# Attention's keys in one part, or in two parts of 640 and 512

## The chip, the cores and the metric

The kernel runs on one core of a Trainium2 chip. A core has five engines that run their own instruction queues in order and signal one another: TensorE (PE: matmuls, with weight loads shown apart as PEld), VectorE (DVE), ScalarE (ACT), GpSimd (POOL) and SyncE (SP), which here only issues DMAs. Results of TensorE land in PSUM, eight banks of 512 fp32 columns on 128 partitions; everything else works in SBUF. The metric is the device time of one execution in microseconds.

## The reference

Three computations follow each other, in fp32:

```python
# attention: B 2, H 8, S 1152, D 64; queries are averaged in pairs, so 576 a head
q_pool = q.reshape(B, H, S // 2, 2, D).mean(axis=3)
scores = scale * np.matmul(q_pool, k.transpose(0, 1, 3, 2))
scores = scores - np.max(scores, axis=-1, keepdims=True)
attn = np.exp(scores)
attn = attn / (np.sum(attn, axis=-1, keepdims=True) + 1e-09)
x = np.matmul(attn, v)          # -> 1152 tokens of 512
# experts: E 4, F 1024, weighted by normed probabilities
out += p[:, e:e + 1] * (np.maximum(x @ w1[e], 0.0) @ w2[e])
# ELU feed-forward: 512 -> 2048 -> 512
g = np.where(h > 0.0, h, np.exp(np.minimum(h, 0.0)) - 1.0)
return g @ w_out
```

## The kernel before

Attention comes first, for 16 heads in 8 pairs. A pair has 2 x 576 = 1152 query rows, cut into 9 blocks of 128; the middle block holds rows of both heads. Queries and keys are split into a rounded part and a remainder, so that products in a fast matmul format keep fp32 precision. The steps have one-letter names in the code, and this document uses them:

- q, k, v: loads (SP); a, b, c: sum, rounded part and remainder of the queries; d, e: the same for keys.
- S: scores of a block, six matmuls of 384 columns into three PSUM banks (`scores`, L401). There are two such buffers, so S of a block waits for E of the block before last.
- R: the negated maximum of a row over its 1152 scores (`max_all`, L412, VectorE). E: the exponential with the row's sum (`exp`, L420, ScalarE), into one of five buffers in SBUF.
- T: three times per block, three 128x128 transposes into one of the two remaining PSUM banks (L431). D and G: the copy out of it into the buffer `pt` (L247, on ScalarE or VectorE).
- V: the product with the values, 18 matmuls of 288 columns (each recorded as two) in three groups (`values`, L453), which holds one of the two banks that the transposes use. O: the copy of its result (L247).
- I: sum plus 1e-9, and its reciprocal (L464, L465, VectorE). 3 and 4: the reciprocals go to DRAM and come back broadcast over 64 partitions (SP). X: the head's result times them (L250, GpSimd). H and L: its rounded part (ScalarE) and remainder (GpSimd), which the experts' matmuls read.

The order on each engine is written by a planner, `order_of`: it takes the steps with their needs from `attention_ops`, durations from the table `STAGES`, and a rank for each, and lays out a schedule; instructions are issued in that order. PSUM banks are given out there too. The experts and the feed-forward (L627 and the lines around it) follow with an order of their own; their first matmuls are mixed in among attention's last.

Of the kernel before, what the change touches and what calls it, by code (L numbers as in the profile page):

```python
# [18 lines left out]
P = 128  # L19
# [8 lines left out]
    "S": (dict(PE=1040), 3),  # L28
    "R": (dict(DVE=1353), 1.5),
    "E": (dict(ACT=1431), 1),  # L30
    "I": (dict(DVE=360), 3),
    "3": (dict(SP=500), 2),
    "4": (dict(SP=500), 2),
    "X": (dict(POOL=1414), 2),
    "T": (dict(PE=327), 2),
    "D": (dict(ACT=480, DVE=557), 2),
    "G": (dict(ACT=480, DVE=557), 2),
    "V": (dict(PE=1900), 2),
    "O": (dict(ACT=720, DVE=750), 1),
    "H": (dict(ACT=690), 0.5),  # L40
    "L": (dict(POOL=1414), -4),
    "a": (dict(POOL=1400), -8),
    "b": (dict(ACT=686), -8),
    "c": (dict(DVE=1400), 5),
    "d": (dict(ACT=1160), -6),
    "e": (dict(POOL=1450), 1),
# [13 lines left out]

MIXED = {"D": dict(ACT=320, DVE=330), "G": dict(ACT=320, DVE=330), "S": dict(PE=2080)}
HALVES = {"a": dict(POOL=690, DVE=373), "b": dict(ACT=375), "c": dict(DVE=373), "d": dict(ACT=575, DVE=373), "e": dict(POOL=1365, DVE=673)}
MB = 9
NP = 5
VC = 3
# [7 lines left out]
def attention_ops(NH, KC):  # L73
# [8 lines left out]
    last = ("V", KC // VC - 1)  # L82
    t = 2700
    for i in range(NH):
# [7 lines left out]
        op(b, [(last[0], i - 3, last[1])] if i > 2 else [], "v", i, after=9000)  # L92

        free = [("S", x) for x in blocks_of(i - 4)] if i > 3 else []
# [8 lines left out]
    for b in range(NB):  # L103
# [30 lines left out]
    for j in range(8):  # L134
        op(w + j, [("S", w + j)], "w", j)
# [7 lines left out]
def order_of(ops):  # L143
# [12 lines left out]
    banks, holds, end, out = {0: 0, 1: 0}, {}, {}, []  # L156

    def ns(o, e):
        return of(o)[e]

    def of(o):
        if o[0] in MIXED and o[1] % MB == 4:
# [4 lines left out]

    while ready:
        best = []
        for o, t in ready.items():  # L170
            if o[0] == "T" or (o[0] == "V" and o[2] == 0):
                if not banks:
                    continue
                t = max(t, min(banks.values()))
            _, e = min((max(t, free[e]) + ns(o, e), e) for e in of(o))
# [3 lines left out]
        free[e] = start + ns(o, e)  # L179
        end[o] = free[e] + LATE.get(o[0], LAG[e])  # L180
        bank = None
        if o[0] == "T" or (o[0] == "V" and o[2] == 0):
            bank = min(banks, key=banks.get)
            del banks[bank]
            holds[o] = bank
        elif o[0] in "DG":
            other = ("DG"[o[0] == "D"], *o[1:])
            if other not in ops or other in end:
                banks[holds[("T", *o[1:])]] = max(end[o], end.get(other, 0))
        elif o[0] == "O":  # L190
# [591 lines left out]
```

## Time and profile before

| | |
|---|---|
| time, median of 3 runs | 900.61 us (899.84 to 901.08) |
| the profiled execution | 903.94 us, its span 901.8 us |
| mean granted clock of TensorE | 0.988 |
| attention, from the profile | 0 to about 299 us |
| busy in the whole span: PE, DVE, ACT, POOL | 866.5, 463.1, 354.3, 395.5 us |

Matmuls are pipelined, and their ends in the profile are modelled: a PE that is shown busy need not be at its peak, and where matmuls follow each other the distance of their starts says more than the duration of one. A row of a group gives the busy time of its instructions, the mean of one, and the idle time of the engine just ahead of them with what ended it.

### The profile page before, as it was taken

The page shows a single profiled execution, that of the slowest core. Times are in us where ns is not written, and L with a number is a line of the kernel's source. Part 1 is how long each engine was busy: PE and PEld are TensorE (multiplying, and loading weights), DVE is VectorE, ACT ScalarE, POOL GpSimd, SP SyncE. Part 2 cuts the span into 40 slices and gives each one's busy share as a digit, 9 for nine tenths or more (in the row PEclk, how much of TensorE's full clock was granted, in tenths as well). Part 3 has the DMA queues.
Part 4 walks back from the last instruction along what each step waited for, and adds up shares of the span by engine and source line. Part 5 has one row for each costly group of instructions (what it writes and reads, how often), then busy time and mean ns, then how long its engine had stood idle before and what let it go on. Part 6 is the DMA issues. An engine that isn't in the chain of part 4 may idle for free.

```text
span 901.8 us, 13389 instructions
## 1 busy us (share of the span) xinstructions
PE 866.5 (96%) x5374; PEld 801.7 (89%) x5374; DVE 463.1 (51%) x601; ACT 354.3 (39%) x609; POOL 395.5 (44%) x278
## 2 busy tenths in 40 slices
PE   7879898989999999999999999999999999999998
PEld 6667666767766899999999999999999999999998
DVE  6737556746544155465464655564656622333333
ACT  5668667767756331312212212212223253313221
POOL 1455444364112351546455554546464573625321
PEclk8989999999999999999999999999999999999999
DMA  8586867588440522424143325233143311000011
GB/s 246 74 166 78 143 74 91 89 157 75 30 24 8 198 105 71 143 55 168 48 143 117 117 95 144 104 105 129 38 156 123 117 48 47 1 1 1 1 40 66
DMA packets 40348, 81.93 MB, mean 91 GB/s; under 512 B 14304, under 2 KB 17376, under 8 KB 37344
## 3 DMA queue, kind: packets, MB, share of 16 engines
q1 hardware_dynamic: 40288, 81.09, 38.5%
q8 instruction: 42, 0.69, 0.4%
q14 instruction: 18, 0.15, 0.1%
HBM read 70.27 MB, written 10.80 MB: 90 GB/s over the span
## 4 chain that ended last, share of the span: by engine, by line
PE 72%; DMA 12%; DVE 4%; ACT 4%; issue 3%; SPq 2%; POOL 2%; ACTq 0%; DVEq 0%; POOLq 0%
PE p L627 62%; DMA q<-in_q 7%; PE t L453 4%; PE s L401 3%; PE t L431 3%; DMA rb<-dr 2%; SPq L321 2%; ACT e L420 2%; DVE nm L412 1%; DMA dr<-sm 1%; DMA k<-in_k 1%; POOL acc L682 1%; ACT pt L247 1%; DVE pt L247 1%; DMA w<-in_wa 1%
## 5 line engine op out<-in xcount | busy, mean ns | idle before, releaser
L627 PE MATMUL p<-XH,h 128*128 128x384 f32 (+1 forms) x608 | 198.4, 326 | 0.4 <-DVE e L657 0.4
L627 PE MATMUL p<-XL,h 128*128 128x384 f32 (+1 forms) x608 | 198.3, 326 | 0.0
L627 PE MATMUL p<-XH,l 128*128 128x384 f32 (+1 forms) x608 | 198.1, 326 | 0.0
L627 PE MATMUL p<-hh,l 128*128 128x384 f32 (+1 forms) x608 | 197.9, 326 | 0.0
L627 PE MATMUL p<-hl,h 128*128 128x384 f32 (+1 forms) x608 | 197.9, 326 | 0.0
L627 PE MATMUL p<-hh,h 128*128 128x384 f32 (+1 forms) x608 | 197.9, 326 | 0.0
L250 POOL TENSOR_TENSOR l<-w,h 128x512 fp32r<-128x512 f32 x96 | 125.6, 1326 | 74.5 <-ACT h L247 73.5
L648 ACT ACTIVATE hh<-p 128x768 fp32r<-128x768 f32 (+1 forms) x50 | 39.5, 789 | 279.9 <-PE p L627 279.9
L649 DVE SCALAR_TENSOR_TENSOR hl<-p,hh 128x768 fp32r<-128x768 f32 (+1 forms) x50 | 46.3, 926 | 161.1 <-ACT hh L648 161.1
L401 PE MATMUL s<-K,Q 128*128 128x384 f32 x480 | 108.2, 365 | 16.2 <-ACT e L420 14.3
L412 DVE TENSOR_REDUCE nm<-s 128x1 f32<-128x1152 f32 x72 | 97.4, 1355 | 47.8 <-PE s L401 47.7
L627 PEld LDWEIGHTS p<-XH,h 128*128 128x128 f32 x608 | 114.1, 188 | 0.7 <-PE p L627 0.7
L627 PEld LDWEIGHTS p<-XL,h 128*128 128x128 f32 x608 | 114.1, 188 | 0.4 <-issue 0.4
L431 PEld LDWEIGHTS t<-ident,e 128*128 128x128 f32 x648 | 75.7, 144 | 43.5 <-issue 15.8
L627 PEld LDWEIGHTS p<-XH,l 128*128 128x128 f32 x608 | 114.1, 188 | 0.0
L627 PEld LDWEIGHTS p<-hh,h 128*128 128x128 f32 x608 | 114.1, 188 | 0.0
L627 PEld LDWEIGHTS p<-hl,h 128*128 128x128 f32 x608 | 114.1, 188 | 0.0
L627 PEld LDWEIGHTS p<-hh,l 128*128 128x128 f32 x608 | 114.1, 188 | 0.0
L431 PE MATMUL t<-ident,e 128*128 128x128 f32 x648 | 101.6, 285 | 13.0 <-ACT pt L247 5.0
L401 PEld LDWEIGHTS s<-K,Q 128*128 128x128 f32 x480 | 85.5, 199 | 21.7 <-ACT e L420 19.3
L601 POOL TENSOR_TENSOR nt<-nt,ne 128x512 f32<-128x512 f32 x32 | 41.8, 1307 | 121.8 <-issue 61.5
L661 POOL TENSOR_TENSOR hl<-e,hh 128x768 fp32r<-128x768 f32 (+1 forms) x26 | 44.9, 1726 | 110.2 <-ACT hh L660 110.1
(52 smaller groups left out, 987.7 us busy)
## 6 DMA issues: line engine op xcount, KB each, us to landing
w<-in_wb SPq DMA_DIRECT2D x8, 1024.0 KB, 6.5
d<-in_va SPq DMA_DIRECT2D x16, 512.0 KB, 4.5
w<-nt SPq DMA_DIRECT2D x32, 256.0 KB, 3.3
d<-in_vb SPq DMA_DIRECT2D x16, 512.0 KB, 4.2
w<-w SPq DMA_DIRECT2D x8, 1024.0 KB, 6.9
q<-in_q SPq DMA_DIRECT2D x56, 144.0 KB, 9.2
k<-in_k SPq DMA_DIRECT2D x56, 144.0 KB, 6.6
w<-in_wa SPq DMA_DIRECT2D x7, 1024.0 KB, 9.6
```

Source lines behind the costliest of these rows:

```text
L247: (nc.scalar.copy if e == "ACT" else engines[e].tensor_copy)(out, a)
L250: engines[e].tensor_tensor(out=out, in0=a, in1=b, op=op)
L321: nc.sync.dma_start(out=t[D * r : D * r + D], in_=src)
L401: nc.tensor.matmul(out=s_t[b][:, j, :KP], lhsT=q[:, x, o : o + P], rhs=ks[p % 2][:, y, KP * j : KP * j + KP], start=k == x == 0, stop=2 * ...
L412: nc.vector.tensor_reduce(out=nm[b], in_=s_t[b][:, :, :KP], axis=AX.XY, op=ALU.max, negate=True)
L431: nc.tensor.transpose(t[:, c * P : c * P + P], et[b % NP][:, (3 * u + c) * P : (3 * u + c + 1) * P], ident)
L453: nc.tensor.matmul(out=tb[i][64 * z : 64 * z + 64, :HQ], lhsT=raws[i, "v"][:, c, :], rhs=pt[i % 2][:, c, half(z)], start=c == 0, stop=c == ...
L601: nc.gpsimd.tensor_tensor(out=t, in0=t, in1=e, op=ALU.add)
L627: nc.tensor.matmul(out=ps, lhsT=w[:, c, m * P : m * P + P], rhs=x[:, c], start=c == 0 and w is hi and x is xh, stop=c == 3 and w is lo,)
L648: nc.scalar.activation(oh, s, AF.Relu)
L649: nc.vector.scalar_tensor_tensor(out=ol, in0=s, scalar=0.0, in1=f(oh), op0=ALU.max, op1=ALU.subtract)
L661: nc.gpsimd.tensor_tensor(out=ol, in0=e, in1=f(oh), op=ALU.subtract)
```

## The change

The 1152 keys are taken in two parts, the first 640 and the other 512. Each part of a block has its own scores (four matmuls of 320 columns into two banks, or two of 512 into one), its own maximum, exponential and sum, and its own PSUM buffer: two buffers of two banks and two of one, six banks as before. The exponentials of a row are thus taken against two different maxima. The values product is split by keys in the same way, into a product of ten and one of eight matmuls with results of their own, each with its own use of a bank and its own copy (O). For each row two factors are made: from the greater of the maxima (`greater`, step I), an exponential (`factors_exp`, step J on ScalarE), and the joined sum's reciprocal (`factors`, step K). They go through DRAM as the reciprocals did, two for each row, and X multiplies both results by them and adds them. The planner's durations and ranks are other ones, and the order of nearly everything in attention differs.

```diff
-    "S": (dict(PE=1040), 3),
...
+    "S": (dict(PE=585), 8),
...
+    "X": (dict(POOL=4240), 0),
...
+SECOND = {"S": dict(PE=455), "R": dict(DVE=690), "E": dict(ACT=790), "V": dict(PE=2140)}
...
-VC = 3
+CUT = 5
+BANKS = {"S0": 2, "S1": 2, "T": 2}
...
-        op(b, need + [b > 1 and ("E", b - 2)], "S", b)
-        op(b, [("S", b)], "R", b)
-        op(b, [("R", b), *[("T", b - NP, u) for u in U if b >= NP]], "E", b)
+        for z in (0, 1):
+            op(b + 0.3 * z, need, "S", b, z)
+            op(b + 0.3 * z, [("S", b, z)], "R", b, z)
+            op(b + 0.3 * z, [("R", b, z), *[("T", b - NP, u) for u in U if b >= NP]], "E", b, z)
         for u in U:
-            op(b, [("E", b)] + [(last[0], i - 2, last[1]) for i in hs if i > 1], "T", b, u)
+            op(b, [("E", b, z) for z in (0, 1) if (z == 0 and 3 * u < CUT) or (z and 3 * u + 3 > CUT)] + [("V", i - 2, 1) for i in hs if i > 1], "T", b, u)
             op(b, [("T", b, u)], "D", b, u)
...
-            for c in range(KC // VC):
-                ds = [("D", x, u) for x in blocks_of(i) for u in U if VC * c < 3 * u + 3 and 3 * u < VC * c + VC]
+            for h in (0, 1):
+                cs = range(CUT, KC) if h else range(CUT)
+                ds = [("D", x, u) for x in blocks_of(i) for u in sorted({c // 3 for c in cs})]
                 if i % 2:
                     ds = [("G", *x[1:]) if x[1] == blocks_of(i)[0] else x for x in ds]
-                op(b + 0.1 * c, ds + [("V", i, c - 1) if c else ("v", i)], "V", i, c)
-            op(b, [("V", i, KC // VC - 1)] + [("L", i - 2)] * (i > 1), "O", i)
-            op(b, [("E", b)], "I", i)
-            op(b, [("I", i), i > 1 and ("4", i - 2)], "3", i)
+                op(b + 0.5 * h, ds + [("V", i, 0) if h else ("v", i)], "V", i, h)
+                op(b + 0.5 * h, [("V", i, h)] + [("L", i - 2)] * (i > 1), "O", i, h)
+            op(b, [("E", b, 0), ("E", b, 1)], "I", i)
+            op(b, [("I", i)], "J", i)
+            op(b, [("J", i)], "K", i)
+            op(b, [("K", i), i > 1 and ("4", i - 2)], "3", i)
             op(b, [("3", i), i % 2 and ("3", i - 1), i > 1 and ("X", i - 2)], "4", i)
-            op(b, [("O", i), ("4", i)], "X", i)
+            op(b, [("O", i, 0), ("O", i, 1), ("4", i)], "X", i)
             op(b, [("X", i)], "H", i)
...
+        PARTS = [(2, CUT * P // 2), (1, (KC - CUT) * P)]
+        s_bank = [
+            [ps_s.tile([P, n, 512], F32, name="s%d%d" % (z, j)) for j in range(BANKS["S%d" % z])]
+            for z, (n, _) in enumerate(PARTS)
+        ]
...
+        st = [[mx_p.tile([P, MB, 2], F32, name="st%d%d" % (j, x), bufs=1) for x in range(3)] for j in range(2)]
+        def part(z):
+            o = CUT * P * z
+            return slice(o, o + PARTS[z][0] * PARTS[z][1])
+        def scores(e, b, z, n):
             p, m = divmod(b, MB)
-            s_t[b] = ps_s.tile([P, 3, 512], F32, tag="s", name="s")
+            s_t[b, z] = t = s_bank[z][n][:, :, : PARTS[z][1]]
             hs = [0] * (m <= MH) + [1] * (m >= MH)
-            n = 2 * len(hs)
+            last = 2 * len(hs) - 1
             q = qs[p % 2].rearrange("p x y q -> p x (y q)")
-            for j in range(3):
+            for j in range(PARTS[z][0]):
+                c = part(z).start + j * PARTS[z][1]
                 for k, y in enumerate(hs):
                     o = P * m - Q * y + QW * y
                     for x in (0, 1):
                         nc.tensor.matmul(
-                            out=s_t[b][:, j, :KP],
+                            out=t[:, j],
                             lhsT=q[:, x, o : o + P],
-                            rhs=ks[p % 2][:, y, KP * j : KP * j + KP],
+                            rhs=ks[p % 2][:, y, c : c + PARTS[z][1]],
                             start=k == x == 0,
-                            stop=2 * k + x == n - 1,
+                            stop=2 * k + x == last,
                         )
-        def max_all(e, b):
-            nm[b] = mx_p.tile([P, 1], F32, tag="nm", name="nm")
+        def max_all(e, b, z):
+            p, m = divmod(b, MB)
+            nm[b, z] = st[p % 2][0][:, m, z : z + 1]
             nc.vector.tensor_reduce(
-                out=nm[b], in_=s_t[b][:, :, :KP], axis=AX.XY, op=ALU.max, negate=True
+                out=nm[b, z], in_=s_t[b, z], axis=AX.XY, op=ALU.max, negate=True
             )
-        def exp(e, b):
+        def exp(e, b, z):
             p, m = divmod(b, MB)
-            if m == 0:
-                sm[p] = x_p.tile([P, MB], F32, tag="sm", name="sm")
             nc.scalar.activation(
-                et[b % NP].rearrange("p (j k) -> p j k", j=3),
-                s_t.pop(b)[:, :, :KP],
+                et[b % NP][:, part(z)].rearrange("p (j k) -> p j k", j=PARTS[z][0]),
+                s_t.pop((b, z)),
                 AF.Exp,
-                bias=nm.pop(b),
-                accum_out=sm[p][:, m : m + 1],
+                bias=nm.pop((b, z)),
+                accum_out=st[p % 2][1][:, m, z : z + 1],
             )
...
+        def stats(i):
+            c = slice(MH + 1, MB) if i % 2 else slice(0, MH + 1)
+            return [t[:, c] for t in st[i // 2 % 2]]
+        def greater(e, i):
+            m, _, t = stats(i)
+            tt("DVE", t[:, :, 0], m[:, :, 0], m[:, :, 1], ALU.min)
+            tt("DVE", t[:, :, 1], t[:, :, 0], m[:, :, 1], ALU.subtract)
+            tt("DVE", t[:, :, 0], t[:, :, 0], m[:, :, 0], ALU.subtract)
+        def factors_exp(e, i):
+            t = stats(i)[2]
+            nc.scalar.activation(t, t, AF.Exp)
+        def factors(e, i):
+            m, s, t = stats(i)
+            tt("DVE", s, s, t, ALU.mult)
+            nc.vector.scalar_tensor_tensor(
+                out=s[:, :, 0], in0=s[:, :, 0], scalar=1e-9, in1=s[:, :, 1], op0=ALU.add, op1=ALU.add
+            )
+            nc.vector.reciprocal(out=s[:, :, 0], in_=s[:, :, 0])
+            for z in (0, 1):
+                tt("DVE", t[:, :, z], t[:, :, z], s[:, :, 0], ALU.mult)
...
+        def values(e, i, h, n):
+            tb[i, h] = bank[n]
+            cs = range(CUT, KC) if h else range(CUT)
+            for c in cs:
                 for z in (0, 1):
                     nc.tensor.matmul(
-                        out=tb[i][64 * z : 64 * z + 64, :HQ],
+                        out=tb[i, h][64 * z : 64 * z + 64, :HQ],
                         lhsT=raws[i, "v"][:, c, :],
                         rhs=pt[i % 2][:, c, half(z)],
-                        start=c == 0,
-                        stop=c == KC - 1,
+                        start=c == cs[0],
+                        stop=c == cs[-1],
...
+        xo = x_p.tile([P, 2, Q], F32, name="xo")
+        fb = x_p.tile([P, 2 * Q], F32, name="fb")
...
+        def output(e, i, h):
+            o = tb.pop((i, h))
             for z in (0, 1):
-                copy(e, xs[i][rows(i), half(z)], o[D * z : D * z + D, :HQ])
+                copy(e, xo[rows(i), h, half(z)], o[D * z : D * z + D, :HQ])
...
+        def factors_out(e, i):
+            p, y = divmod(i, 2)
+            if y == 0:
+                rc[p] = dr_p.tile([MB, P, 2], F32, tag="dr", name="dr")
+            s = slice(MH + 1, MB) if y else slice(0, MH + 1)
+            nc.sync.dma_start(out=rc[p][s].rearrange("m p z -> p m z"), in_=stats(i)[2])
+        def factors_in(e, i):
+            p, y = divmod(i, 2)
+            d = rc[p].rearrange("m p z -> (m p z)")[2 * Q * y : 2 * Q * y + 2 * Q]
+            nc.sync.dma_start(out=fb[rows(i)], in_=d.unsqueeze(0).to_broadcast([D, 2 * Q]))
         def x_scaled(e, i):
-            tt(e, xs[i][rows(i)], xs[i][rows(i)], rc.pop((i, "b"))[rows(i)], ALU.mult)
+            x = xo[rows(i)]
+            tt(e, x, x, fb[rows(i)].rearrange("p (q z) -> p z q", z=2), ALU.mult)
+            tt(e, x[:, 0], x[:, 0], x[:, 1], ALU.add)
```

TensorE's queue around the first head's values product, before (`t_104`, `t_105` are the two banks, `e_97` to `e_101` the five buffers of exponentials, `s` a score buffer):

```order
L401 MATMUL s<-K_108,Q_106 128x384 x6
L431 MATMUL t_104<-ident,e_101 128x128 x3
L453 MATMUL t_105<-pt_102,v 64x288 x6
L431 MATMUL t_104<-ident,e_97 128x128 x3
L453 MATMUL t_105<-pt_102,v 64x288 x6
L431 MATMUL t_104<-ident,e_97 128x128 x3
L453 MATMUL t_105<-pt_102,v 64x288 x6
L431 MATMUL t_104<-ident,e_97 128x128 x3
L401 MATMUL s<-K_108,Q_106 128x384 x6
L431 MATMUL t_105<-ident,e_98 128x128 x3
L431 MATMUL t_104<-ident,e_98 128x128 x3
L401 MATMUL s<-K_109,Q_107 128x384 x6
```

And at the same head with the change (`s_106`, `s_107` are the buffers of the first part, `s_108`, `s_109` of the second):

```order
L442 MATMUL s_107<-K_112,Q_110 128x320 x4
L496 MATMUL t_105<-ident,e_97 128x128 x3
L519 MATMUL t_104<-pt_102,v 64x288 x10
L496 MATMUL t_105<-ident,e_97 128x128 x3
L442 MATMUL s_109<-K_112,Q_110 128x512 x2
L442 MATMUL s_106<-K_112,Q_110 128x320 x4
L496 MATMUL t_104<-ident,e_97 128x128 x3
L442 MATMUL s_108<-K_112,Q_110 128x512 x2
L496 MATMUL t_105<-ident,e_98 128x128 x3
L496 MATMUL t_104<-ident,e_98 128x128 x3
L442 MATMUL s_107<-K_113,Q_111 128x320 x4
L496 MATMUL t_105<-ident,e_98 128x128 x3
```

The three values groups with transposes between them are now one of ten matmuls here and one of eight further on, and scores stand in half blocks between the transposes.

VectorE's queue at the reciprocals of one head, before (`nm` the maximum, `sm` the sums):

```order
L412 TENSOR_REDUCE nm<-s 128x1 x3
L247 COPY pt_102<-t_105 128x3x128
L464 TENSOR_SCALAR sm<-sm 128x5
L465 RECIPROCAL sm<-sm 128x5
L412 TENSOR_REDUCE nm<-s 128x1 x2
```

And at the first head's factors with the change (`st_114`, `st_115`, `st_116` hold maxima, sums and factors):

```order
L278 TENSOR_TENSOR st_116<-st_114 128x5
L278 TENSOR_TENSOR st_116<-st_116,st_114 128x5 x2
L453 TENSOR_REDUCE st_114<-s_106 128x1
L275 COPY pt_102<-t_105 128x3x128
L275 COPY pt_103<-t_104 128x3x64
L453 TENSOR_REDUCE st_114<-s_108 128x1
L278 TENSOR_TENSOR st_115<-st_115,st_116 128x10
L486 SCALAR_TENSOR_TENSOR st_115<-st_115 128x5
L489 RECIPROCAL st_115<-st_115 128x5
L278 TENSOR_TENSOR st_116<-st_116,st_115 128x5 x2
```

Two instructions in one place have become eight in two groups, with ScalarE's exponential (J) between the groups.

## Rows read from the trace of the kernel before

**Rows 1.** Stretches: us, busy time (count) of each engine, PEclk, DMA share, GB/s

```profile
0.00:299.00 299.00, 267.39 (x1741) 203.08 (x1742) 170.68 (x233) 198.62 (x372) 110.89 (x84) 0.97 0.63 95
299.00:902.00 603.00, 599.12 (x3635) 598.60 (x3633) 292.40 (x368) 155.68 (x238) 284.64 (x194) 1.00 0.27 89
```

**Rows 2.** Groups of the first 299 us: busy us, mean ns | idle before, releasers

```profile
L431 PE MATMUL t<-ident,e 128*128 128x128 f32 x648 | 101.6, 285 | 13.0 <-ACT pt L247 5.0 <-DVE pt L247 3.1 <-ACT x L247 2.3
L412 DVE TENSOR_REDUCE nm<-s 128x1 f32<-128x1152 f32 x72 | 97.4, 1355 | 47.8 <-PE s L401 47.7
L420 ACT ACTIVATE e<-s,nm 128x1152 f32<-128x1152 f32 x72 | 88.0, 1225 | 4.7 <-DVE nm L412 4.0
L464 DVE TENSOR_SCALAR sm<-sm 128x5 f32<-128x5 f32 (+1 forms) x16 | 7.5, 472 | 1.7 <-ACT e L420 1.7
```

**Rows 3.** Waits (us, times, longest); then the timeline at the longest and another

```profile
PEld s L401 <- ACT e L420: 19.3, 20, 3.8
...
44.99 0.68 ACT L366 ACTIVATE Q<-q 128x576 fp32r<-128x576 f32 x1 [4.26 <-DMA q<-in_q]
...
46.93 1.54 PEld L401 LDWEIGHTS s<-K,Q 128*128 128x128 f32 x6 [3.84 <-ACT e L420]
...
275.35 1.01 PEld L401 LDWEIGHTS s<-K,Q 128*128 128x128 f32 x6 [1.19 <-ACT e L420]
```

**Rows 4.** Timeline behind a values product: start, us, instruction, idle before

```profile
221.67 1.30 PE L401 MATMUL s<-K,Q 128*128 128x384 f32 x6
...
223.01 1.36 DVE L412 TENSOR_REDUCE nm<-s 128x1 f32<-128x1152 f32 x1 [0.43 <-PE s L401]
...
223.39 1.29 PE L401 MATMUL s<-K,Q 128*128 128x384 f32 x6
...
224.66 1.22 ACT L420 ACTIVATE e<-s,nm 128x1152 f32<-128x1152 f32 x1
...
226.02 1.00 PEld L401 LDWEIGHTS s<-K,Q 128*128 128x128 f32 x6 [0.93 <-ACT e L420]
226.03 1.32 PE L401 MATMUL s<-K,Q 128*128 128x384 f32 x6 [0.69 <-ACT e L420]
...
227.75 2.33 PE L401 MATMUL s<-K,Q 128*128 128x384 f32 x12
```

**Rows 5.** Timeline inside a values product

```profile
199.29 1.68 PE L453 MATMUL t<-pt,v 128*64 128x288 f32 x12
...
200.90 0.55 PE L431 MATMUL t<-ident,e 128*128 128x128 f32 x3
...
201.38 1.68 PE L453 MATMUL t<-pt,v 128*64 128x288 f32 x12
```

**Rows 6.** Lines L247, L464, L465, L374 (ns min/median/max); a timeline at 72 us

```profile
L247 ACT COPY pt<-t x141: 309/479/494, 17.2 to 294.2; 128x384 f32<-128x384 f32 x115, 128x192 f32<-128x192 f32 x26
L247 DVE COPY pt<-t x99: 341/549/560, 14.5 to 290.8; 128x384 f32<-128x384 f32 x77, 128x192 f32<-128x192 f32 x22
...
L464 DVE TENSOR_SCALAR sm<-sm x16: 154/172/1399, 26.2 to 283.2; 128x5 f32<-128x5 f32 x8, 128x4 f32<-128x4 f32 x8
...
L465 DVE RECIPROCAL sm<-sm x16: 179/185/191, 27.6 to 283.4; 128x5 f32<-128x5 f32 x8, 128x4 f32<-128x4 f32 x8
...
L374 DVE SCALAR_TENSOR_TENSOR Q<-q,Q x18: 451/750/1796, 6.1 to 214.5; 128x576 fp32r<-128x576 f32 x14, 128x288 fp32r<-128x288 f32 x4
...
72.56 1.41 POOL L250 TENSOR_TENSOR XL<-x,XH 64x576 fp32r<-64x576 f32 x1 [4.65 <-ACT XH L247]
72.80 1.80 DVE L374 SCALAR_TENSOR_TENSOR Q<-q,Q 128x576 fp32r<-128x576 f32 x1
```

**Rows 7.** Timeline where attention ends: the last head's X and H, the first ReLU

```profile
299.64 1.42 POOL L250 TENSOR_TENSOR x<-x,rb 64x576 f32<-64x576 f32 x1 [6.98 <-ACT x L247]
...
301.10 0.67 ACT L247 CAST XH<-x 64x576 fp32r<-64x576 f32 x1 [1.53 <-POOL x L250]
301.79 0.65 ACT L648 ACTIVATE hh<-p 128x576 fp32r<-128x576 f32 x1
```

More of the change, by code (lines that the diff above doesn't have):

```diff
@@ L81, in attention_ops @@
     U = range(3)
-    last = ("V", KC // VC - 1)
     t = 2700
@@ L91, in attention_ops @@
             op(b, old, "k", i)
-        op(b, [(last[0], i - 3, last[1])] if i > 2 else [], "v", i, after=9000)
-        free = [("S", x) for x in blocks_of(i - 4)] if i > 3 else []
+        op(b, [("V", i - 3, 1)] if i > 2 else [], "v", i, after=9000)
+        free = [("S", x, z) for x in blocks_of(i - 4) for z in (0, 1)] if i > 3 else []
         for z in zs:
@@ L134, in attention_ops @@
     for j in range(8):
-        op(w + j, [("S", w + j)], "w", j)
+        op(w + j, [("S", w + j, 0)], "w", j)
     for j in range(4):
@@ L155, in order_of @@
     free = dict.fromkeys(LAG, 0)
-    banks, holds, end, out = {0: 0, 1: 0}, {}, {}, []
-    def ns(o, e):
-        return of(o)[e]
+    banks = {x: dict.fromkeys(range(n), 0) for x, n in BANKS.items()}
+    holds, end, out = {}, {}, []
     def of(o):
+        if o[0] == "S" and o[1] % MB == 4:
+            return {e: 2 * n for e, n in (SECOND["S"] if o[2] else STAGES["S"][0]).items()}
+        if o[0] in SECOND and o[2]:
+            return SECOND[o[0]]
         if o[0] in MIXED and o[1] % MB == 4:
@@ L166, in of, with takes, gives @@
         return STAGES[o[0]][0]
+    def takes(o):
+        return "S%d" % o[2] if o[0] == "S" else "T" if o[0] in "TV" else None
+    def gives(o):
+        x, *k = o
+        if x in "DG" and (("DG"[x == "D"], *k) not in ops or ("DG"[x == "D"], *k) in end):
+            return ("T", *k), max(end[o], end.get(("DG"[x == "D"], *k), 0))
+        if x in "OE":
+            return ("SV"[x == "O"], *k), end[o]
     while ready:
@@ L170, in order_of @@
         for o, t in ready.items():
-            if o[0] == "T" or (o[0] == "V" and o[2] == 0):
-                if not banks:
+            x = takes(o)
+            if x:
+                if not banks[x]:
                     continue
-                t = max(t, min(banks.values()))
-            _, e = min((max(t, free[e]) + ns(o, e), e) for e in of(o))
+                t = max(t, min(banks[x].values()))
+            _, e = min((max(t, free[e]) + n, e) for e, n in of(o).items())
             best.append((max(t, free[e]), ops[o][1], o, e))
@@ L178, in order_of @@
         del ready[o]
-        free[e] = start + ns(o, e)
+        free[e] = start + of(o)[e]
         end[o] = free[e] + LATE.get(o[0], LAG[e])
[L181 to L190, printed above, removed]
-            banks[holds[("V", o[1], 0)]] = end[o]
+        x, bank = takes(o), None
+        if x:
+            bank = min(banks[x], key=banks[x].get)
+            del banks[x][bank]
+            holds[o] = x, bank
+        back = gives(o)
+        if back:
+            x, n = holds.pop(back[0])
+            banks[x][n] = back[1]
         out.append((start, len(out), o, e, bank))
@@ L519, in attention_then_moe_then_elu_ffn @@
         do = dict(
-            S=scores, R=max_all, E=exp, I=recip, X=x_scaled, T=transposes, V=values, O=output,
+            S=scores, R=max_all, E=exp, I=greater, J=factors_exp, K=factors, X=x_scaled, T=transposes, V=values, O=output,
             H=x_high, L=x_low, q=load_q, k=load_k, v=load_v, a=q_sum, b=q_high, c=q_low,
@@ L526, in attention_then_moe_then_elu_ffn @@
         )
[L527 removed]
+        do.update({"3": factors_out, "4": factors_in})
         with tc.manual_schedule():
@@ L542, in attention_then_moe_then_elu_ffn @@
             for (x, *k), e, n in order_of(attention_ops(NH, KC)):
-                if x == "T" or (x == "V" and k[1] == 0):
-                    do[x](e, *k, n)
-                elif x == "V":
-                    do[x](e, *k, None)
-                else:
-                    do[x](e, *k)
-            assert not s_t and not xs
+                do[x](e, *k, *([] if n is None else [n]))
+            assert not s_t
     bc_p = ctx.enter_context(tc.tile_pool(name="bc", bufs=1))
```

79 lines of the change are left out of this document (30 added, 49 removed).

## The prediction

> **What bounds the kernel now.** I read the stretches first: the attention stage ends at 299 us, and behind it TensorE is busy for 599.1 of 603 us [rows 1]. The change doesn't touch that second part, so whatever it is worth must come out of the first 299 us or the seam between the two. In those, TensorE shows 267 us busy, ScalarE 199, VectorE 171, GpSimd 111, at a mean granted clock of 0.97 [rows 1]. No engine is full; TensorE is the nearest, so next I looked for what it waits for.
>
> The view of waits gives 19.3 us in 20 pieces in which the weight loads of the score matmuls wait for the exponential (E) [rows 3]. They are of two kinds. Four are above 1 us, from 3.84 us down to 1.19, 10.0 us together (the first and the last of them: [rows 3]); at the largest, ScalarE itself stood in front of a query that had not landed [rows 3]. The other 16 are 9.3 us together, and the timeline shows how one is made [rows 4]: the score matmuls of a block start at 221.67, its maximum (R) at 223.01, E at 224.66, and the scores of the block after next, which need the same three PSUM banks, at 226.03, 4.36 us after the first. TensorE has transposes and one other block to do meanwhile, and that is 0.93 us too little on the loads' row. So the round trip of a score buffer is a limit just behind a head's values product, where the pipeline refills.
>
> **The change part by part.**
>
> *Score buffers.* Scores, maximum and exponential go in two parts, and each part's bank goes round by itself. Six matmuls of 384 columns become four of 320 and two of 512: 2304 columns both times and six loads, so nothing for TensorE. Six take 1.04 us (twelve 2.33 less six 1.29, [rows 4]); four of 320 take 0.58 by columns. Trip of the first part: 0.58 and the 0.30 until R starts, R at 0.80, 0.29 to E, E at 0.77, 0.15 to the next scores: 2.9 us against 4.36. That is 1.4 us less, more than 0.93, so all 16 short waits go. TensorE's own row shows 0.69 where the loads' row shows 0.93 [rows 4], so I take 9.3 x 0.74 = **-7 us**. What is late next there is the copy of a transpose out of its bank. The four long waits stay: what they wait for is not made sooner.
>
> *Values product.* In three stretches with transposes between, a V stretch takes 1.61 us and the three transposes behind it 0.48 (199.29, 200.90, 201.38, [rows 5]); elsewhere six transposes take 1.72 - 1.04 = 0.68 us (pitch of two score groups, [rows 4]), 0.34 for three. So each change between the two costs 0.14. Two stretches instead of three save one to two changes a head: 16 x 1.5 x 0.14 = **-3 us**.
>
> *VectorE.* Copies of 384 and 192 columns at 549 and 341 ns [rows 6] give 1.083 ns an element; a maximum over 1152 at 1355 ns [rows 2] leaves 107 ns fixed, paid once more for each of 72 blocks: +8 us. Eight small instructions a head instead of two, 0.15 to 0.22 each (the least that one took is 0.154, [rows 6]): +19 us. The copies out of the values bank double to 64; the new order puts 38 on VectorE, at 288 columns between the 341 and 549 ns: +17 us. It also gets 7 whole and 7 half transposes' copies more: +6. Sum 171 + 50 = 221 of 299 us. The idle time was 128 us, of which 47.8 lay ahead of a maximum, where it waited for scores [rows 2]; at 221 busy 78 are left, and in the same proportion 29 us ahead of maxima. That is the cover that hides delays of VectorE.
>
> *Waits of VectorE for GpSimd.* The trace shows a VectorE instruction on SBUF held until a GpSimd instruction ends: at 72.80 one took 1.80 us beside a GpSimd subtraction from 72.56 to 73.97, against a median of 0.75 [rows 6]. The old small instruction, L464, took 7.5 us in 16 against 0.154 at best: 5.0 us of holding, 0.31 each [rows 2, 6]. GpSimd's share rises by 156/111 (below). If of each head's two groups only the first instruction is held, that is 16 x 2 x 0.31 x 1.4 = 14 us; if all seven but the reciprocal are, 49. I take 14, because a group may run on once it has started: the reciprocals behind L464 took 0.18 to 0.19 each time [rows 6]. Under the cover of 29 it would cost nothing; as delays are not spread evenly I put **+2 us**, with ends 0 and +20 (49 less 29).
>
> The Trainium skill (SBUF — State Buffer, "SBUF: two separate sides") says that VectorE and GpSimd share a port pair as an exclusive lock, held for the whole instruction, taken by a VectorE instruction that has two SBUF inputs or runs in a two-port mode. By that rule seven of the eight new instructions can be held, which speaks for 49 rather than 14; the trace agrees for the two forms it has [rows 6] and has no tensor_tensor of this kind beside a busy GpSimd.
>
> *ScalarE.* Copies at 479 and 309 ns [rows 6] give 0.885 ns an element, so E at 1225 ns [rows 2] has 205 fixed: +15 us for 72, and up to +29 if the reading of the sum is not covered any more. One small exponential a head: +4. Less the copies that moved: -8. 199 becomes 210 of 299; hidden under its 100 us of idle time: 0, at most +5.
>
> *GpSimd.* The scaling X takes 1.42 us for 576 elements [rows 7]; now 1152 and an addition of 576: +2.8 us, 16 times, 111 to 156 us of 299. Behind it in its queue stand the query sums and key differences of a later pair, which have a pair's time: 0.
>
> *SyncE.* The write of the factors is issued after two more hops, and the broadcast read carries twice the bytes; behind them stand loads of queries and keys. One long wait the more would be +3.8 [rows 3]; I take 0, ends -4 and +4.
>
> *The seam.* The last head's X ran from 299.64, its rounding (H) on ScalarE at 301.10, and behind that in ScalarE's queue stands the first ReLU, at 301.79 [rows 7]. With X 2.8 us longer that ReLU starts near 304.6, and TensorE has only two result buffers to fill meanwhile: 0 to +2.8, **+1.5 us**.
>
> Sum: -7 - 3 + 2 + 1.5 = -6.5 us on the profiled execution: 903.9 - 6.5 = 897.4. The median of the runs is 3.3 us below that execution, so **894 us**.
>
> **The rivals.**
>
> *VectorE held at every small instruction (slower).* Place: the group of factors, between maxima. Price: 49 us of holding less the cover of 29 is +20, with -10 and +1.5 is +11.5: 912 us. It decides from about 38 us of holding on (29 + 10 - 1.5). For it: GpSimd goes from 37% to 52% of the stage, often in unbroken rows, and a maximum stands right behind the factors. Against: nothing behind L464 was held, and the values product gives TensorE 2 us of work that needs no VectorE.
>
> *The gain is given back at the transposes' banks (no change).* Scores come sooner, and the same order then waits for copies out of two banks; copies on VectorE queue behind more maxima. Then the 7 us are lost and -3 + 2 + 1.5 = +0.5 is left: 901 us. For it: TensorE already waits for these copies, 8.1 us in the stage [rows 2]. Against: half blocks of scores between transposes give the copies time.
>
> *The long waits go too (a larger gain).* The whole order is written anew. If the 10.0 us of long waits go with the short: 894 - 10 = 884 us. For it: such waits come from an order that counts on a load too early. Against: loads are no sooner.
>
> **How the numbers follow.** Forecast 0.40, its own range 888 to 900; held VectorE 0.30; given back 0.15; larger gain 0.15. About 0.2%, 1.8 us, is what can be told from no change. Faster: 0.34 of the first, all of the last, 0.02 of the third: 0.51. Slower: 0.29 of the second and 0.06 of the others: 0.35. Same 0.14. The range goes from the larger gain with its ends on ScalarE and SyncE (884 - 6) to a little past the held VectorE: 878 to 915.
>
> **What would show it.** Right: scores' waits for E under half of 19.3 us, each left above 1 us; maxima about 0.80 and 0.66 us; VectorE near 235 us busy in the stage; the stage ends near 293. Wrong: small tensor_tensor instructions with a mean above 0.45 us and a VectorE beyond 255 us (the first rival); waits of transposes for copies well above 8.1 us (the second); a first ReLU that stands more than 3 us behind the last values (the seam).

## The result, and the profile after

The changed kernel took 911.59 us (median of 4 runs, 908.92 to 913.19), the kernel before in the same comparison 900.23 us (898.79 to 901.08). The ratio is 1.0125, its 95% interval 1.0097 to 1.0153: slower, where 894 us had been forecast. The profiled execution took 911.97 us with a span of 910.3 us.

The same two stretches as in [rows 1], columns as there (length; busy time and count of PE, PEld, DVE, ACT, POOL; granted clock; DMA share; GB/s):

```profile
0.00:299.00 299.00, 260.19 (x1696) 196.07 (x1698) 237.76 (x452) 208.50 (x503) 150.81 (x100) 0.94 0.44 103
299.00:910.00 611.00, 605.31 (x3680) 601.76 (x3676) 292.33 (x368) 158.05 (x243) 292.83 (x198) 1.00 0.27 88
```

By 299 us TensorE has issued 1696 matmuls where it was at 1741 before. VectorE is busy for 237.8 us instead of 170.7 (221 were forecast, and 235 given as the mark of the forecast), the clock fell from 0.97 to 0.94, and the DMA share, which the prediction did not read, fell from 0.63 to 0.44 while more bytes moved.

The groups of attention (busy us, mean ns | idle before, releasers), to be set against [rows 2]:

```profile
L496 PE MATMUL t<-ident,e 128*128 128x128 f32 x648 | 106.1, 289 | 32.4 <-DVE pt L275 24.3 <-ACT pt L275 4.9 <-DVE xo L275 2.9
...
L453 DVE TENSOR_REDUCE st<-s 128x1 f32<-128x640 f32 (+1 forms) x144 | 104.9, 749 | 8.7 <-PE s L442 7.7 <-ACT XH L275 0.3
...
L278 DVE TENSOR_TENSOR st<-st,st 128x5 f32<-128x5 f32 (+2 forms) x80 | 36.1, 469 | 1.9 <-ACT st L481 0.3
...
L278 DVE TENSOR_TENSOR st<-st 128x5 f32<-128x5 f32 (+1 forms) x16 | 8.7, 545 | 0.0
...
L486 DVE SCALAR_TENSOR_TENSOR st<-st 128x5 f32<-128x5 f32 (+1 forms) x16 | 5.1, 318 | 0.6
...
L489 DVE RECIPROCAL st<-st 128x5 f32<-128x5 f32 (+1 forms) x16 | 3.0, 186 | 0.5
```

The maxima cost what they should (0.749 us in the mean of both sizes). The last four groups are the eight small instructions of each head: 52.9 us; how much of that is holding, the experiments tell. The idle time ahead of a maximum, which was to be the cover for delays of VectorE, shrank from 47.8 to 8.7 us, and the idle time of the transposes rose from 13.0 to 32.4 us, 24.3 of it for copies on VectorE. The two lines that hold the small instructions, one by one (ns min/median/max):

```profile
L278 DVE TENSOR_TENSOR st<-st,st x80: 150/166/5127, 23.7 to 290.5; 128x5 f32<-128x5 f32 x32, 128x4 f32<-128x4 f32 x32, 128x10 f32<-128x10 f32 x8, 128x8 f32<-128x8 f32 x8
...
L489 DVE RECIPROCAL st<-st x16: 179/186/192, 27.9 to 290.2; 128x5 f32<-128x5 f32 x8, 128x4 f32<-128x4 f32 x8
```

Half of the 80 take 166 ns or less, and the longest 5127; the reciprocal, with one input, is never late. The timeline at the longest hold (start, length, instruction, idle time before it):

```profile
199.14 2.52 POOL L278 TENSOR_TENSOR l<-w,h 128x512 fp32r<-128x512 f32 x2
...
200.49 5.13 DVE L278 TENSOR_TENSOR st<-st,st 128x5 f32<-128x5 f32 x1
...
201.61 1.41 POOL L278 TENSOR_TENSOR XL<-xo,XH 64x576 fp32r<-64x576 f32 x1
202.96 1.41 POOL L278 TENSOR_TENSOR q<-q 128x576 f32<-128x576 f32 x1
204.31 1.27 POOL L278 TENSOR_TENSOR l<-w,h 128x512 fp32r<-128x512 f32 x1
205.53 1.41 POOL L278 TENSOR_TENSOR q<-q 128x576 f32<-128x576 f32 x1
...
205.65 1.32 DVE L278 TENSOR_TENSOR st<-st,st 128x5 f32<-128x5 f32 x1
...
206.89 0.54 DVE L275 COPY pt<-t 128x384 f32<-128x384 f32 x1
...
207.49 0.50 PEld L496 LDWEIGHTS t<-ident,e 128*128 128x128 f32 x3 [6.92 <-DVE pt L275]
```

Two subtractions of 128x5 follow each other. The first is the longest of the list above. It starts at 200.49, while the second of the two `l` in the first row runs (to 201.66), and is held through that one and through `XL`, `q` and `l`, four GpSimd instructions without a gap; it ends at 205.61, where the last of these ends (205.58). The second is held through the next `q` and ends with it, at 206.97. Behind the subtractions stands the copy of a transpose, and TensorE's weight loads stand still for 6.9 us. A hold through a row like this is the exception: of the 112 small instructions with two inputs, 29 took more than 0.25 us, the longest 5.1, two more 2.2 and 2.5, and all others at most 1.6 us, about the length of one GpSimd instruction. The granted clock is 1.00 before, 0.84 over 198 to 207 us, and 0.51 (the lower of the two levels) from 207 to 211:

```profile
198.00:207.00 9.00, 3.00 (x21) 2.42 (x19) 8.91 (x6) 2.79 (x7) 8.94 (x7) 0.84 0.51 146
207.00:211.00 4.00, 3.51 (x15) 3.40 (x16) 3.06 (x10) 2.24 (x6) 0.00 (x0) 0.51 0.00 0
```

So a long wait is paid again in the clock behind it. The Trainium skill (SBUF — State Buffer, "SBUF: two separate sides") has the lock that explains a hold: whichever of the two engines starts first keeps the shared ports for its whole instruction. The trace agrees: all three groups with two inputs have late ones (the longest 5.1, 1.6 and 1.4 us), each of the 29 ends within 0.04 us of the end of a GpSimd instruction, and the reciprocal with one input is never late. In the timeline above, three GpSimd instructions started while the subtraction was already waiting.

The waits of the stage (us, times, longest), for [rows 3], and the seam, for [rows 7]:

```profile
PEld t L496 <- DVE pt L275: 31.6, 26, 6.9
...
ACT st L481 <- DVE st L278: 19.7, 11, 6.1
...
PEld s L442 <- ACT e L459: 5.4, 14, 0.9
```

```profile
312.19 0.67 ACT L275 CAST XH<-xo 64x576 fp32r<-64x576 f32 x1 [5.16 <-POOL xo L278]
312.88 0.65 ACT L705 ACTIVATE hh<-p 128x576 fp32r<-128x576 f32 x1
...
314.38 0.19 PEld L684 LDWEIGHTS p<-XH,h 128*128 128x128 f32 x1 [2.19 <-DVE hl L706]
```

Scores wait for E 5.4 us instead of 19.3, and no wait above 1 us is left: the four long ones went, and 14 short ones are left. The first ReLU stands behind a longer X as forecast, and costs TensorE 2.2 us. And the loads land sooner; before, and then after (DMA queue with packets, MB and share; issues with KB each and median us to landing; 0 to 260 us):

```profile
q1 hardware_dynamic: 23667, 27.61, 69.8%
...
q<-in_q SPq DMA_DIRECT2D x56, 144.0 KB, 9.2
...
dr<-sm SPq DMA_DIRECT2D x7, 2.5 KB, 10.4
```

```profile
q1 hardware_dynamic: 23040, 29.34, 47.0%
...
q<-in_q SPq DMA_DIRECT2D x56, 144.0 KB, 3.0
...
dr<-st SPq DMA_DIRECT2D x7, 5.0 KB, 4.6
```

### The profile page after: what moved, and what is told of

It is laid out like the page before. It is cut to its first block, busy times and chain, and to the rows that moved or that the text cites. A ratio compares the mean times of both kernels' runs of the same rounds, so it can differ in the third digit from the quotient of the medians.

```text
span 910.3 us, 13830 instructions
## 1 busy us (share of the span) xinstructions
PE 865.5 (95%) x5374; PEld 797.8 (88%) x5374; DVE 530.1 (58%) x820; ACT 366.6 (40%) x746; POOL 443.6 (49%) x298
## 4 chain that ended last, share of the span: by engine, by line
PE 79%; DVE 11%; issue 3%; ACT 2%; POOL 2%; DMA 1%; SPq 0%; DVEq 0%; ACTq 0%; POOLq 0%
PE p L684 60%; PE t L519 8%; PE s L442 6%; PE t L496 5%; DVE st L278 4%; DVE st L453 3%; DVE pt L275 2%; POOL acc L739 1%; ACT e L459 1%; ACT pt L275 1%; DMA k<-in 1%; POOL l L278 1%; DVE xo L275 1%; POOL xo L278 0%; DVE nt L643 0%
## 5 line engine op out<-in xcount | busy, mean ns | idle before, releaser
L496 PE MATMUL t<-ident,e 128*128 128x128 f32 x648 | 106.1, 289 | 32.4 <-DVE pt L275 24.3
L496 PEld LDWEIGHTS t<-ident,e 128*128 128x128 f32 x648 | 79.5, 146 | 59.1 <-DVE pt L275 31.6
L442 PE MATMUL s<-K,Q 128*128 128x320 f32 (+1 forms) x480 | 120.2, 372 | 4.2 <-DVE K L278 2.3
L453 DVE TENSOR_REDUCE st<-s 128x1 f32<-128x640 f32 (+1 forms) x144 | 104.9, 749 | 8.7 <-PE s L442 7.7
L459 ACT ACTIVATE e<-s,st 128x640 f32<-128x640 f32 (+1 forms) x144 | 106.4, 747 | 7.9 <-DVE st L453 7.5
```

Of the source, the lines that this page charges most:

```text
L442: nc.tensor.matmul(out=t[:, j], lhsT=q[:, x, o : o + P], rhs=ks[p % 2][:, y, c : c + PARTS[z][1]], start=k == x == 0, stop=2 * k + x == last,)
L453: nc.vector.tensor_reduce(out=nm[b, z], in_=s_t[b, z], axis=AX.XY, op=ALU.max, negate=True)
L459: nc.scalar.activation(et[b % NP][:, part(z)].rearrange("p (j k) -> p j k", j=PARTS[z][0]), s_t.pop((b, z)), AF.Exp, bias=nm.pop((b, z)), ...
L496: nc.tensor.transpose(t[:, c * P : c * P + P], et[b % NP][:, (3 * u + c) * P : (3 * u + c + 1) * P], ident)
```

## The experiments

Two questions: does the holding of small two-input instructions make the kernel slower, and what would it gain without? The theory was that every two-input instruction is held and that this, through the copies of transposes, is the whole loss. The rivals: VectorE's larger amount of work, the second values product, the new order. Times are medians; a ratio is against runs of the kernel before on the same chip, where that took 897.95 to 905.97 us.

**No two-input instructions.** As many small instructions at the same places, each with one input; the factors are not computed.

```diff
-            tt("DVE", t[:, :, 0], m[:, :, 0], m[:, :, 1], ALU.min)
+            nc.vector.reciprocal(out=t[:, :, 0], in_=m[:, :, 0])
...
-                tt("DVE", t[:, :, z], t[:, :, z], s[:, :, 0], ALU.mult)
+                nc.vector.reciprocal(out=t[:, :, z], in_=s[:, :, 0])
```

> The changed kernel with its seven small two-input VectorE instructions a head replaced by reciprocals, which have one input; their number, places and needs stay, the factors are not computed. Theory (held): the small instructions of the changed kernel took 53 us against some 21 at their fastest, and TensorE's waits for copies by VectorE grew to 24 us because of it; without holding they take 16 x 8 x 0.19 = 24 us, those waits fall under 10 us, and the time falls by 12 to 18 us, to 894 to 900. Rival (work): what costs is the greater number of instructions on VectorE (maxima, factors, copies), which stays: 909 to 913. Rival (order): TensorE waits for copies because the new order leaves them too little time: waits stay above 20 us, 907 to 913.

872.34 us, ratio 0.9616 (0.9598 to 0.9633). The first 299 us, and one of the groups of small instructions:

```profile
0.00:299.00 299.00, 286.36 (x1978) 224.05 (x1979) 218.23 (x468) 219.21 (x527) 174.27 (x116) 0.98 0.48 119
```

```profile
L485 DVE RECIPROCAL st<-st 128x10 f32<-128x10 f32 (+1 forms) x16 | 3.2, 200 | 0.0
```

The 128 instructions take 21.4 us together, so 52.9 - 21.4 = 31.5 us of the changed kernel were holding. Without it the ratio falls from 1.0125 to 0.9616, by 5.1% or 46 us of 900. VectorE is still busy for 218 us: its work is not the loss. But the rest gains far more than the 8.5 us that were forecast for it.

**A short scaling on GpSimd.** X works on 8 columns of 576; the rest of the results stays unscaled.

```diff
+            w = slice(0, 8)
-            tt(e, x, x, fb[rows(i)].rearrange("p (q z) -> p z q", z=2), ALU.mult)
+            tt(e, x[:, :, w], x[:, :, w], fb[rows(i)].rearrange("p (q z) -> p z q", z=2)[:, :, w], ALU.mult)
```

> The changed kernel with GpSimd's scaling of the results cut from 576 to 8 columns, so that most of the output is not scaled; VectorE's instructions stay as they are. Theory (held): GpSimd is busy some 62 us less in attention, the small two-input instructions are held less, from 53 us to 30 to 40 in all, and the time falls by 5 to 12 us, of which 2 at the seam. Rival (work) and rival (order): 2 us from the seam and no more, 908 to 911.

892.95 us, ratio 0.9848 (0.9822 to 0.9874).

```profile
L278 DVE TENSOR_TENSOR st<-st,st 128x5 f32<-128x5 f32 (+2 forms) x80 | 24.2, 320 | 1.9 <-ACT st L481 0.3
```

With the two groups behind it (7.6 and 6.2) and the reciprocal (3.0), the small instructions take 41.0 us: 12 us less holding, with the same instructions on VectorE. The time falls by 2.8%, 25 us where 5 to 12 were expected; the shorter seam can be 2 of them. What else a shorter GpSimd frees isn't separated here.

**The two kinds put into the kernel before.** Seven more small instructions a head on scratch data, with two inputs, or with one.

```diff
+            tt("DVE", t[:, :, 0], s, s, ALU.min)
...
+                tt("DVE", t[:, :, z], t[:, :, z], s, ALU.mult)
```

```diff
+            for z in (0, 1, 0, 1, 0, 1, 0):
+                nc.vector.reciprocal(out=t[:, :, z], in_=s)
```

> The kernel before, in its own order, with seven small two-input VectorE instructions a head on scratch ahead of the sum's reciprocal. Theory (held): GpSimd is busy 111 us of the stage instead of 154, so 16 x 7 instructions take more than their 18 us, 30 to 50, with single ones above 2 us, and the time rises by 3 to 10 us. Rival (work): they take their 18 us, and the time rises by no more than the kernel with seven reciprocals does.

> The kernel before with seven small reciprocals a head on scratch at the same place: the same number of instructions with one input each. Theory (held): they take 16 x 7 x 0.19 = 21 us, none is held, and VectorE's idle time covers them: within 2 us of before. Rival (work): 3 to 10 us slower, as with two inputs.

With two inputs 924.17 us, ratio 1.0186 (1.016 to 1.0213); with one 905.56 us, ratio 0.9999 (0.9972 to 1.0027). The added instructions and the one behind them, first of the one kernel, then of the other:

```profile
L250 DVE TENSOR_TENSOR scr<-scr,sm 128x5 f32<-128x5 f32 (+1 forms) x80 | 20.3, 278 | 1.6
...
L250 DVE TENSOR_TENSOR scr<-sm 128x5 f32<-128x5 f32 (+1 forms) x16 | 6.6, 410 | 1.7 <-ACT e L420 1.7
...
L250 DVE TENSOR_TENSOR scr<-scr 128x10 f32<-128x10 f32 (+1 forms) x16 | 3.9, 242 | 0.5
...
L473 DVE TENSOR_SCALAR sm<-sm 128x5 f32<-128x5 f32 (+1 forms) x16 | 2.7, 172 | 0.5
```

```profile
L468 DVE RECIPROCAL scr<-sm 128x5 f32<-128x5 f32 (+1 forms) x112 | 13.3, 168 | 1.7 <-ACT e L420 1.7
...
L469 DVE TENSOR_SCALAR sm<-sm 128x5 f32<-128x5 f32 (+1 forms) x16 | 5.9, 369 | 0.6
```

112 small instructions cost nothing; given two inputs they take 17.5 us more, and the kernel 17 us more. The addition of 1e-9 behind them (L464 of before) is held less in the first kernel, by 3 us, so 14 us of holding stand for 17 us of time, where 3 to 10 had been expected. The theory holds in a kernel that has no other part of the change. But the number of inputs is not the whole rule. That addition has one input, as the reciprocals have, and in the second kernel, right behind them, it took up to 1.12 us, where none of the 112 reciprocals took more than 0.19. Why it is held and they are not, no run here shows.

**The factors on GpSimd.** Both factors are made; the two-input steps run on GpSimd, the lesser maximum as a reduction on VectorE. In the second version the reciprocal is GpSimd's too, as a power of -1.

```diff
-            tt("DVE", t[:, :, 0], m[:, :, 0], m[:, :, 1], ALU.min)
+            nc.vector.tensor_reduce(out=t[:, :, 0], in_=m, axis=AX.X, op=ALU.min)
...
+            tt(e, s[:, :, 0], s[:, :, 0], minus[:, : s.shape[1]], ALU.pow)
```

> The changed kernel, all of it computed, with every two-input instruction of the factors on GpSimd, the lesser of the negated maxima by a one-input reduction and the reciprocal on VectorE; the planner lays out a new order for it. Theory (held): no small instruction of VectorE is held, TensorE's waits for copies by VectorE fall below 10 us, and the kernel is 2 to 4% faster than before. Rival (the order of the changed kernel is bad by itself, and leaving the factors out helped by freeing the other engines): within 1% of before.

> As the last one, with the reciprocal on GpSimd too (a power of -1), so that VectorE does one reduction for the factors and waits for nothing of theirs. Theory (held): as fast as the last one or up to 1% faster. Rival (GpSimd's queue: small instructions there come behind scalings of 2.7 us, and ScalarE's exponential of the factors waits for them): 1% or more slower than the last one, with ScalarE's waits for GpSimd above 15 us.

879.6 us, ratio 0.9714 (0.9654 to 0.9773), and 877.69 us, ratio 0.9687 (0.9627 to 0.9746). In the second:

```profile
L280 POOL TENSOR_TENSOR st<-st,minus 128x5 f32<-128x5 f32 (+1 forms) x16 | 18.0, 1124 | 1.3
...
L280 POOL TENSOR_TENSOR st<-st,st 128x5 f32<-128x5 f32 (+2 forms) x80 | 15.5, 203 | 21.1 <-DVE st L479 14.5 <-ACT st L488 3.0
```

On GpSimd the 80 small instructions take 203 ns in the mean and 213 at most, so they are not held there (the 21.1 us ahead of them are waits for their data); the power takes 1124 ns. TensorE's matmuls wait 2.3 and 1.7 us for copies by VectorE in the two versions, where it was 24.3. Both versions beat both kernels; their intervals overlap, and the second has the lowest median of those that make both factors.

**One values product; no addition.** The kernel without two-input instructions, with one product of 18 and one copy (the scaling as long as before, the second result left out); and the kernel before without its addition of 1e-9.

> The changed kernel with reciprocals for the seven two-input instructions, as in the first of these runs, and the values product whole again: 18 matmuls in one bank, one copy a head, GpSimd's scaling as long as before it; factors and the second result are left out. If the gain comes from the score buffers' parts, it stays within 1% of the kernel with two products (0.96 of before). If the values product's parts bring it, by shorter holds of the transposes' bank and fewer changes between products and transposes, it is 1% or more slower than that one.

> The kernel before without the addition of 1e-9 to the sums, the one small instruction that its trace shows held (5.0 us in all). Theory (held): 1 to 6 us faster than before, since a hold costs TensorE a lower clock and a late copy too. Rival (such holds lie in idle time): within 1 us.

871.2 us, ratio 0.9617 (0.9569 to 0.9665): the split of the product neither brings nor costs anything that can be told within the half per cent of that interval. 902.02 us, ratio 0.9972 (0.9943 to 1.0): the 5 us of holding at L464 are worth 0 to 5 us, which says little.

**The transfers of the factors.** What remained open was a gain of 34 us (905.97 - 872.34) where 8.5 had been forecast, and a write to DRAM that landed in less than half the time. First the kernel before, with each reciprocal made and written twice side by side; then the kernel without two-input instructions, with the transfers of before; then the new ranks alone, in the kernel before.

```diff
-                rc[p] = dr_p.tile([MB, P], F32, tag="dr", name="dr")
+                rc[p] = dr_p.tile([MB, P, 2], F32, tag="dr", name="dr")
...
-            nc.sync.dma_start(out=rc[p][s].rearrange("m p -> p m"), in_=sm[p][:, s])
+            nc.sync.dma_start(out=rc[p][s].rearrange("m p z -> p m z"), in_=sp[p][:, s])
```

> The kernel before, in which only the shape of the reciprocals' transfers is that of the changed kernel: each reciprocal is made twice, the write to DRAM goes in elements of 8 bytes instead of 4 (as many elements, twice the bytes), and the broadcast read carries two numbers a query. Theory that the loads are faster because of the wider elements: the write lands in about 4.5 us instead of 10.4, loads of queries and keys in 3 to 4 us instead of 9.2 and 6.6, the waits of the score matmuls above 1 us (10.0 us together) go, and the time is 8 to 12 us shorter than before. Rival, that loads land sooner because the new order issues them at better moments: the write still takes about 10 us, loads too, and the time is within 2 us of before or up to 3 us longer, since SyncE moves twice the bytes.

> The changed kernel without two-input instructions on VectorE (as in the run that took 872 us) and with the transfers of the kernel before: one factor a query, written in elements of 4 bytes and read back at half the length; both scalings use it. The second factor is left out. Theory of the wider elements: the write lands in about 10 us again, loads of queries and keys in 7 to 9 us, and the time rises by 8 to 12 us over 872. Rival, the order: it stays within 2 us of 872, with loads at 3 to 4 us.

> The kernel before, in which only the planner's ranks of the steps that both kernels have are those of the changed kernel; every instruction is as before, its place in the queues is not. Theory that the order by itself brings much of the 34 us by which the changed kernel without two-input instructions beats the kernel before: 8 to 20 us shorter than before, with fewer waits of scores for exponentials (19.3 us before). Rival, that the split of the keys brings them: within 3 us of before, or longer, since those ranks were made for half blocks.

Wide transfers in the kernel before: 885.66 us, ratio 0.9776 (0.9735 to 0.9817). Narrow ones in the other: 884.93 us, ratio 0.9757 (0.9724 to 0.979), which by the two ratios is 12.7 us above the same kernel with wide ones. The ranks: 908.47 us, ratio 1.0026 (1.0006 to 1.0047). So the new ranks alone bring nothing, and the transfers are worth 13 to 20 us. Queue and issues of the kernel before with wide transfers (0 to 260 us), and its score waits:

```profile
q1 hardware_dynamic: 24528, 30.23, 53.2%
...
q<-in_q SPq DMA_DIRECT2D x56, 144.0 KB, 5.6
...
dr<-sp SPq DMA_DIRECT2D x8, 5.0 KB, 4.9
```

```profile
PEld s L401 <- ACT e L421: 11.3, 18, 1.2
```

The waits above 1.2 us are gone, as the theory had it. The median landing of the loads is not what tells the kernels apart, though. With the ranks alone the writes still take 10.4 us, and the loads land as soon as with wide transfers, without a gain in time:

```profile
q<-in_q SPq DMA_DIRECT2D x56, 144.0 KB, 5.5
```

What tells them apart is how long the engines wait for these loads, all of them together: 32.6 us before, 27.6 with the ranks alone (the longest 12.1), 10.2 with wide transfers (the longest 3.1). GpSimd's waits for a query, with narrow and with wide transfers in the changed kernel without two-input instructions (28.3 us before):

```profile
POOL q L278 <- DMA q<-in_q: 26.3, 6, 9.9
```

```profile
POOL q L278 <- DMA q<-in_q: 5.7, 3, 2.6
```

What a narrow write does shows in the kernel before. It is issued at 114.80 us; three stretches of 3 us behind it, and one after it:

```profile
116.00:119.00 3.00, 3.00 (x24) 1.66 (x21) 0.00 (x0) 1.46 (x5) 1.49 (x2) 1.00 0.88 12
119.00:122.00 3.00, 3.00 (x23) 2.94 (x22) 2.16 (x3) 1.95 (x5) 1.52 (x2) 1.00 0.85 43
122.00:125.00 3.00, 2.31 (x17) 2.04 (x16) 2.16 (x3) 2.84 (x6) 1.28 (x1) 1.00 0.67 22
...
128.00:131.00 3.00, 3.00 (x23) 1.96 (x21) 2.93 (x5) 2.72 (x5) 1.61 (x2) 1.00 1.07 287
```

For some 9 us the DMA engines are busy to 67 to 88% and move 12 to 43 GB/s; afterwards, as busy, 287. What shows as busy are the loads that were issued behind the write, from 115.21 us on: the write's own packets are all recorded by 116.1 us, while 25 packets of these loads, 2304 bytes each, took 1.5 to 6.9 us (the median of such packets in this kernel is 0.12 us). So one write of 2 to 2.5 KB seems to hold up everything behind it; by what, the trace does not show.

**Size of an element, or spacing.** The last run writes only one of the two, so 4 bytes again, but 8 bytes apart.

```diff
-            nc.sync.dma_start(out=rc[p][s].rearrange("m p z -> p m z"), in_=sp[p][:, s])
+            nc.sync.dma_start(out=rc[p][s].rearrange("m p z -> p m z")[:, :, 0], in_=sp[p][:, s, 0])
```

> The kernel before with the paired layout of the reciprocals in DRAM (8 bytes a query, read back at twice the length, as in the run that took 885.7 us), but only one reciprocal of a pair is written: elements of 4 bytes, 8 bytes apart. The other halves are zeroed once, by two small extra writes in the first two pairs. It tells the size of an element from the spacing. Theory that the size of an element decides (a write of 4 bytes is dear, one of 8 is not): the write lands in about 10 us again, loads of queries in 8 to 10 us, DMA share near that of before, and the time is 900 to 908 us where before is 905. Rival, that the spacing decides (neighbouring 4-byte writes collide): the write lands in 5 us, and the time is 884 to 890 us.

886.93 us, ratio 0.9883 (0.9855 to 0.9912; the kernel before was at 897.95 us on this chip), and

```profile
q1 hardware_dynamic: 26864, 30.22, 51.8%
...
dr<-sp SPq DMA_DIRECT2D x8, 2.5 KB, 4.3
```

The write of the same 2.5 KB in the same 4-byte elements lands in 4.3 us instead of 10.4. For the landing, spacing decides, not size; my own theory of the two was the wrong one. The gain in time is 1.2% here, against 2.2% with pairs, although the two kernels differ by 1.3 us: the kernel before was faster on this chip. Two things stay open: why neighbours of 4 bytes are so dear, and what part the read has, which is twice as long in every wide version.

## Why the prediction was wrong

**The step that failed** is "Waits of VectorE for GpSimd": 14 us of holding taken, +2 us for it. The holding was 31.5 us, between its ends of 14 and 49, and its removal is worth 46 us (0.9616 against 1.0125), beyond its upper end of +20. Two of its reasons fell. "A group may run on once it has started" was read from a reciprocal, which is held in no run; it says nothing of the others: of the 29 late ones 13 stand first in their group and 16 behind. And the cover of 29 us was an average: a hold lasts until GpSimd lets go, up to 5.1 us for one instruction, and the copy that TensorE needs next stands behind it. No idle time ahead of maxima elsewhere helps there. Part of the price above 31.5 us is the clock, 0.94 of the stage against 0.98 without holds: on 260 us of busy TensorE that is an estimate of 260 x 0.04 / 0.98 = 11 us.

**The first rival** named 912 us, and the time was 911.6. Its mechanism is the right one: small tensor_tensor instructions at 0.47 us in the mean, late ones at six of the eight places, the loss that way round. Its sum is right only by luck. It had 49 us of holding and 29 of cover on top of a gain of 8.5; in truth a loss of 46 stands against a gain of 35 (0.0384 of 900). By its own terms the 31.5 us of holding that came, fewer than the 38 from which it was to decide, would have slowed nothing, and its other sign, a VectorE beyond 255 us, did not come (237.8).

**Score buffers** (-7) and **SyncE** (0, ends -4 and +4) were mis-sized. "The four long waits stay: what they wait for is not made sooner" was false, and so was that all the short ones would go: the long ones went, and 14 short ones with 5.4 us are left. In the kernel before, with nothing changed but the transfers of the reciprocals and a second copy of each, the longest wait is 1.2 us instead of 3.8. By the two comparisons these transfers are worth 13 to 20 us. The chain of waits of the kernel before had shown it: 7% of the span, some 63 us, ran through loads of queries, and I read only the waits of TensorE.

```profile
PE p L627 62%; DMA q<-in_q 7%; PE t L453 4%; PE s L401 3%; PE t L431 3%; DMA rb<-dr 2%; SPq L321 2%; ACT e L420 2%; DVE nm L412 1%; DMA dr<-sm 1%; DMA k<-in_k 1%; POOL acc L682 1%; ACT pt L247 1%; DVE pt L247 1%; DMA w<-in_wa 1%
```

With narrow transfers and no holds the changed kernel still gains 2.4%, 22 us, where -7 - 3 + 1.5 had been forecast. The ranks alone bring nothing, and the split product nothing that can be told. What is left is the split of the scores with the order that it allows, and the addition at L464, which that kernel doesn't have (0 to 5 us above). I counted the short waits of the scores; why the split is worth more than they are was not taken apart.

**Values product** (-3): not to be found, within some 4 us either way. **VectorE** (+50 us busy, hidden): right in its parts, maxima at 0.749, and 218 us busy in the kernel without holds, which took 872 us. **ScalarE** (210 forecast, 208.5) and **GpSimd** (156, 150.8): right. **The seam** (+1.5): 2.2. **Given back at the transposes' banks**: the waits for copies did rise, from 8.1 to 29.2 us, but behind held instructions, not behind maxima; without holds they are 5.0 us:

```profile
PE t L494 <- DVE pt L275: 3.5, 9, 0.7
...
PE t L494 <- ACT pt L275: 1.5, 5, 0.5
```

## What to carry to other kernels

Before small two-input instructions are put on VectorE, look at how long GpSimd runs without a gap at that place: that row, not their own 0.16 us, is what each can cost, and it is paid by whatever stands behind them. Give them a form that ran free here (the reciprocal, or a reduction, which took 0.17 us at most; the addition with one input did not), or put them on GpSimd itself. And where DMA engines are busy while few bytes move, look for a small write to neighbouring addresses before counting on a load's time.

## What the runs showed of the hardware that was not expected

- A waiting VectorE instruction can be passed over by GpSimd's next ones: 5.1 us for one of 0.16 us, through four GpSimd instructions in a row, three of which started while it waited.
- An instruction with one input can be held too: the addition of 128x5 took up to 1.12 us behind reciprocals at the same place that never took more than 0.19.
- 31.5 us of holding cost 46 us in this kernel, and 14 us cost 17 in the kernel before.
- A write of 640 4-byte elements to neighbouring addresses in DRAM, from different partitions, took 10.4 us, and behind one of this kind the DMA engines were 67 to 88% busy at 12 to 43 GB/s; 8 bytes apart the elements took 4.3 us, and with 8 bytes each 4.9 us.
